# A retention layer with a token mixer: batch 0 loaded pair by pair, with two tokens to a partition

## Chip, cores, metric

The kernel runs on one core of a Trainium2 chip. The metric is the device time of one execution in microseconds (us), as the median of several runs. Lower is better.

## What is computed

The inputs q, k and v have the shape (4 batches, 8 heads, 768 tokens, 64 features) in float32. The first half is a retention recurrence. In each head a 64x64 state decays by a factor gamma that depends on the head, takes up the outer product of k and v of the token, and is read out with q:

```python
for t in range(S):
    state = gamma * state + einsum('bhd,bhe->bhde', k[:, :, t], v[:, :, t])
    y[:, :, t] = scale * einsum('bhd,bhde->bhe', q[:, :, t], state)
```

The heads of a token are then laid side by side to a row x of 512 features, and the second half mixes tokens within a batch and projects:

```python
wq, wk = x @ w_q, x @ w_k                       # 512 -> 64
W_tok  = scale2 * einsum('bsd,btd->bst', wq, wk)
mixed  = einsum('bst,btd->bsd', W_tok, x)
out    = maximum(mixed, 0) @ w_out              # 512 -> 512
```

The mixing needs no S x S matrix: z = wk^T x is a 64x512 matrix for each batch, and mixed = wq z. So no output of a batch can be made before z is complete, that is before all tokens of that batch have passed through the first half.

## The kernel before

**Chunks, pairs, batches.** The 768 tokens of a batch are six chunks of 128 (C), and two chunks are a pair (p). There are twelve pairs in all, 0 to 2 for batch 0, 3 to 5 for batch 1, and so on (NP = 3 pairs to a batch). Inside a chunk the recurrence is done as attention: scores from k and q, a causal mask, and a product with v ("intra"). Between chunks the state carries over ("inter"). The decay is folded into k and q when they are cast to bf16: k is multiplied by gamma^-t (table `fk`), q by gamma^t (table `fq`).

**Steps.** Each step is a small function, with the pair and often the chunk as its arguments:

- `ck`, `cq`, `cv` (lines 300 to 313, with `decay`, 286): cast a pair of k, q or v from its staging tile to bf16, with the decay for k and q. This runs on DVE (V), POOL (P) or ACT (A).
- `trk`, `trq` (315, 330): eight TensorE transposes of a pair of k or q into one PSUM bank; `ekT`, `eqT` evict them to SBUF.
- `sc` (349): scores of a chunk, eight matmuls that contract over the 64 features of one head (64 rows of the array, 128 columns), two heads side by side on the two row halves. `eat` (365) evicts them, with the mask on DVE, or without it on ACT followed by `msk` (380) on POOL.
- `st` (420): adds a chunk's k^T v to the state in PSUM, four matmuls on 128 rows. `es` (433) evicts the state to bf16.
- `in` (390) and `ia` (405): inter and intra part of y in one PSUM bank; `ia` has eight matmuls on 128 rows. `ex` (448) evicts y as x.
- `xt`, `exT`, `wqk`, `ew` (455 to 496): transpose x, project it with w_q and w_k, evict.
- `za`, `zm`, `ez` (515 to 525): z of a batch, twelve matmuls in a column-tiled form (64 output rows each).
- `mx`, `r`, `pj`, `eo` (527 to 565): mix, relu, output projection (line 553, four matmuls of 512 columns), eviction, and then the store of the pair.
- `W`, `WO`: cast the weights.

**The order.** Nothing is scheduled by the compiler. The string `ORDER` (line 18) is walked token by token (line 583) and lays down the instructions of each engine in that order. In `sc.1.0@2+3` the numbers are pair, chunk and PSUM banks; `ekT.5:A` runs on ACT. An engine takes its instructions strictly in order, so that a step that waits holds back all that stands behind it on the same engine. `fill.150` puts 150 matmuls on a zero tile, which nobody reads, ahead of the next step on PE (`fresh`, line 277). The order before has fills of 150, 36, 5 and 3.

**The loads.** All DMAs are issued by SP, in program order. `load` (155) brings one tensor of a whole batch (1.57 MB). k and v come with token n*128+p on partition p, in rows of 256 bytes; q with the tokens 2p and 2p+1 of a pair on partition p, in rows of 512 bytes. At the start come k, q, v of batch 0, w_q, w_k, k of batch 1, w_out, q and v of batch 1. The third cast of a tensor of batch b issues its load for batch b+2 (`release`, 186) into the same staging tile. In the old order all of these loads stand before the first store on SP.

Of the kernel before, what the change touches and what calls it, by code (L numbers as in the profile page):

```python
# [9 lines left out]
FP32 = mybir.dt.float32  # L10
# [16 lines left out]
ew.0:V ia.2.0 es.2.0:V xt.1@6 ex.2.0:A exT.1:V fill.5 in.2.1@4
ia.2.1 ck.4:P ex.2.1:V wqk.1@5 WO:V trk.5@4 ew.1:A xt.2@6
ekT.5:A za.0@5 ck.3:P exT.2:V trk.4@2 wqk.2@4 ekT.4:A ew.2:V
trk.3@6 zm.0 ekT.3:V ez.0:A mx.0@4+5 cq.3:P mx.1@6+2 r.0.0:A  # L30
r.0.1:V r.1.1:A r.1.0:V mx.2@4+5 pj.0.1@2 cq.5:P trq.3@6 eo.0.1:A
eqT.3:V pj.0.0@2 cq.4:P trq.5@6 r.2.0:A sc.3.0@0+1 eqT.5:V r.2.1:A
pj.1.0@4 cv.3:A eat.3.0:V cv.5:P trq.4@5 cv.4:A pj.2.0@6 eqT.4:V
eo.1.0:V st.3.0 eo.0.0:A ia.3.0@5 eo.2.0:V es.3.0:A sc.3.1@0+1 sc.4.0@2+3
ex.3.0:A pj.2.1@4 eat.3.1:V in.3.1@5 eo.2.1:A st.3.1 eat.4.0:V ia.3.1
es.3.1:A fill.3 sc.4.1@0+1 pj.1.1@4 ex.3.1:A eat.4.1:V ck.6:P st.4.0
in.4.0@5 es.4.0:A xt.3@6 eo.1.1:V sc.5.0@0+1 exT.3:V st.4.1 ck.7:P
sc.5.1@2+3 es.4.1:A eat.5.0:V wqk.3@4 st.5.0 ew.3:A in.5.0@6 es.5.0:V
ia.4.0 ck.8:P ia.5.0 ex.4.0:A trk.7@4 eat.5.1:V ex.5.0:A in.4.1@5
ia.4.1 in.5.1@6 ex.4.1:A ekT.7:V ia.5.1 cq.6:P trk.8@2 ex.5.1:A  # L40
xt.4@4 ekT.8:V xt.5@5 exT.4:A trk.6@6 exT.5:V cq.7:P trq.6@2
ekT.6:V wqk.4@4 eqT.6:V wqk.5@5 ew.4:A cq.8:P trq.7@4 ew.5:A
cv.6:A sc.6.1@0+1 eqT.7:V sc.6.0@2+3 zm.1@5 eat.6.1:V cv.8:A cv.7:P
trq.8@4 st.6.0 eat.6.0:V ez.1:A sc.7.0@0+1 eqT.8:A mx.3@5+6 es.6.0:V
r.3.1:A sc.7.1@2+3 ia.6.0@4 r.3.0:A eat.7.1:V in.6.1@6 st.6.1 ex.6.0:A
ia.6.1 pj.3.0@5 es.6.1:A ex.6.1:V ck.10:P in.7.0@4 ck.9:P eo.3.0:A
st.7.0 xt.6@6 es.7.0:A eat.7.0:V exT.6:V sc.8.1@0+1 sc.8.0@2+3 in.7.1@5
eat.8.0:V st.7.1 trk.10@6 es.7.1:A ia.7.0 ia.7.1 eat.8.1:V ex.7.0:A
st.8.0 wqk.6@2 ex.7.1:A ck.11:P trk.9@4 es.8.0:A ew.6:V in.8.0@5
ekT.9:V ia.8.0 in.8.1@2 ex.8.0:A ia.8.1 pj.3.1@4 ekT.10:V cq.9:P  # L50
ex.8.1:A trk.11@5 eo.3.1:A xt.7@6 ekT.11:V xt.8@4 cq.10:P exT.7:V
trq.9@2 exT.8:A wqk.7@5 eqT.9:V wqk.8@4 cq.11:P ew.7:A cv.11:A
trq.10@6 ew.8:V mx.4@5+2 eqT.10:V sc.9.0@0+1 r.4.0:A zm.2@4 eat.9.0:V
r.4.1:A cv.10:P trq.11@5 cv.9:A sc.10.1@2+3 ez.2:A eqT.11:V sc.9.1@0+1
pj.4.0@6 eat.9.1:V st.9.0 eo.4.0:A pj.4.1@4 eat.10.1:V es.9.0:A sc.11.0@0+1
eo.4.1:A mx.5@5+6 eat.11.0:V sc.11.1@2+3 r.5.0:A in.9.1@4 st.9.1 ia.9.0@5
es.9.1:A ia.9.1 r.5.1:V sc.10.0@0+1 ex.9.0:A eat.11.1:V st.10.0 pj.5.0@6
es.10.0:A ex.9.1:A in.10.1@5 eat.10.0:V st.10.1 eo.5.0:A pj.5.1@2 es.10.1:A
eo.5.1:A xt.9@4 in.11.0@6 exT.9:V st.11.0 ia.11.0 es.11.0:A ia.10.1
ex.11.0:V wqk.9@4 ex.10.1:A in.11.1@2 ew.9:A ia.11.1 mx.6@5+6 ex.11.1:A  # L60
in.10.0@4 r.6.0:V ia.10.0 r.6.1:A xt.11@2 ex.10.0:A pj.6.1@5 exT.11:V
wqk.11@4 eo.6.1:A mx.7@6+2 ew.11:V xt.10@5 r.7.0:A r.7.1:V pj.6.0@4
exT.10:V pj.7.0@6 eo.6.0:A wqk.10@4 eo.7.0:A pj.7.1@5 ew.10:A mx.8@4+6
eo.7.1:A za.3@2 r.8.0:A zm.3 r.8.1:V ez.3:A pj.8.0@4 eo.8.0:A
mx.9@5+6 pj.8.1@2 r.9.1:V r.9.0:A pj.9.0@4 eo.8.1:A mx.10@5+6 eo.9.0:A
pj.9.1@2 r.10.1:V r.10.0:A mx.11@4+5 eo.9.1:A pj.10.0@6 r.11.1:V r.11.0:A
pj.11.1@2 eo.10.0:V pj.10.1@5 eo.11.1:A pj.11.0@4 eo.10.1:V eo.11.0:A
""".split()

# [5 lines left out]
def kernel(  # L75
# [9 lines left out]
):  # L85

# [65 lines left out]

    staged = {}

    def load(name, b):
        src = {"k": k, "q": q, "v": v}[name]
        if name == "q":
            t = buf("q_st", b % 2, [H, NP, 2, D], FP32)
            nc.sync.dma_start(
                out=t.rearrange("p h n j d -> p (h n) (j d)"),  # L160
                in_=src[b].rearrange("h (n p j) d -> p (h n) (j d)", p=128, j=2),
            )
        else:
            t = buf(name + "_st", b % 2, [H, NCH, D], FP32)
            nc.sync.dma_start(
                out=t.rearrange("p h n d -> p (h n) d"),
                in_=src[b].rearrange("h (n p) d -> p (h n) d", p=128),
            )
        staged[name, b] = t
# [459 lines left out]
```

## Time and profile before

| | us |
|---|---|
| median of 3 runs (lowest, highest) | 110.6 (109.92, 110.98) |
| the profiled execution | 110.53 |
| its span, from first to last instruction | 108.7 |
| PE busy in the span | 95.0 (87%) |
| DVE, ACT, POOL busy | 74.4, 61.2, 52.6 |
| mean granted TensorE clock | 0.972 |
| DMA | 26.66 MB, 245 GB/s on average |

Busy times are sums of an engine's instructions. PE is the matmul part of TensorE and PEld its weight loads; matmuls are pipelined, so that a single one shows a longer duration than the step from one to the next. The chain that ended last follows the last instruction back to what released it at each step, and its durations are the steps from one to the next. SPq rows are DMA issues on SP's queue; their duration is the time for which the issue holds SP, and the DMA view gives the time from issue to landing.

### The profile page before, as it was taken

To read this page: it belongs to the slowest core of one execution; us is meant where nothing else is said; L and a number is where in the kernel's file an instruction comes from. 1 tells how busy PE (TensorE), PEld (TensorE's weight loads), DVE (VectorE), ACT (ScalarE), POOL (GpSimd) and SP (SyncE) were. 2 spreads that over 40 slices of the span, in tenths; PEclk is the share of its full clock that TensorE was granted. 3 is DMA by queue.
4 is the path that set the end of the run, shared out by engine and by line. 5 is a ranking of instruction groups with operands and counts; after the bars stand their busy time and mean duration, and the time that the engine had idled before them with its cause. 6 is when DMAs were issued, how large, how long until landed. Compare 5 with 4: busy or idle time off the path is not lost.

```text
span 108.7 us, 3189 instructions
## 1 busy us (share of the span) xinstructions
PE 95.0 (87%) x1362; PEld 72.7 (67%) x1362; DVE 74.4 (68%) x97; ACT 61.2 (56%) x112; POOL 52.6 (48%) x46
## 2 busy tenths in 40 slices
PE   6999984669997679999999899999999999999920
PEld 6999982449895435666998678888675965633400
DVE  2007999998599544999976999966998556132520
ACT  6000003494427146985785985868789974767420
POOL 6607355299696993185999059999000000000000
PEclk9999999995999999999999999999999999999995
DMA  1989995599999979699998899798013220444472
GB/s 19 320 266 346 353 337 148 154 328 236 383 390 344 330 233 332 193 369 342 301 319 258 284 347 304 241 409 344 18 71 128 111 87 0 193 193 193 193 295 91
DMA packets 19020, 26.66 MB, mean 245 GB/s; under 512 B 1472, under 2 KB 13760, under 8 KB 19008
## 3 DMA queue, kind: packets, MB, share of 16 engines
q1 hardware_dynamic: 19008, 26.48, 73.5%
q8 instruction: 10, 0.16, 0.6%
q14 instruction: 2, 0.02, 0.0%
HBM read 20.19 MB, written 6.29 MB: 243 GB/s over the span
## 4 chain that ended last, share of the span: by engine, by line
PE 69%; DVE 18%; ACT 6%; issue 2%; DVEq 0%; ACTq 0%
PE bank_ps L553 14%; PE bank_ps L280 11%; PE duo_ps L553 5%; PE bank_ps L473 5%; PE duo_ps L355 5%; PE state_ps L424 4%; PE bank_ps L411 4%; PE bank_ps L396 4%; DVE at L371 4%; DVE qs L288 4%; PE bank_ps L532 3%; PE bank_ps L336 3%; DVE wout_sb L146 3%; PE bank_ps L460 3%; PE bank_ps L319 2%; DVE kT L146 2%
## 5 line engine op out<-in xcount | busy, mean ns | idle before, releaser
L288 POOL TENSOR_TENSOR ks<-k_st,fk 128x1024 bf16<-128x1024 f32 x10 | 19.9, 2004 | 14.7 <-PE state_ps L424 6.6
L371 DVE TENSOR_TENSOR at<-duo_ps,cmask 128x1024 bf16<-128x1024 f32 x21 | 25.0, 1216 | 0.1
L288 POOL TENSOR_TENSOR qs<-q_st,fq 128x1024 bf16<-128x1024 f32 x10 | 19.8, 2008 | 4.2 <-DMA q_st<-in_q_dram 4.2
L553 PE MATMUL bank_ps<-wout_sb,relu 128*128 128x512 bf16 x72 | 18.2, 380 | 0.1
L280 PE MATMUL bank_ps<-warm 128*128 128x128 bf16 x191 | 14.0, 247 | 1.0 <-DVE warm L196 1.0
L280 PEld LDWEIGHTS <-warm 128*128 128x128 bf16 x194 | 13.8, 113 | 1.0 <-DVE warm L196 1.0
L553 PEld LDWEIGHTS <-relu 128*128 128x128 bf16 x96 | 8.1, 97 | 9.1 <-issue 1.2
L144 ACT CAST x<-bank_ps 128x512 bf16<-128x512 f32 x18 | 10.4, 590 | 3.7 <-PE bank_ps L411 3.4
L144 ACT CAST s_sb<-state_ps 64x256 bf16<-64x256 f32 x28 | 10.3, 367 | 3.9 <-PE state_ps L424 2.8
L355 PE MATMUL duo_ps<-qT,kT 64*128 64x128 bf16 x192 | 8.8, 219 | 2.7 <-ACT at L144 1.5
L547 DVE TENSOR_SCALAR relu<-bank_ps 128x512 bf16<-128x512 f32 x8 | 5.4, 689 | 8.3 <-PE bank_ps L532 8.3
L144 ACT COPY o<-bank_ps 128x512 f32<-128x512 f32 x13 | 7.6, 586 | 6.1 <-PE bank_ps L553 6.1
L144 ACT COPY qT<-bank_ps 128x1024 bf16<-128x1024 bf16 x2 | 2.0, 1018 | 14.3 <-PE bank_ps L336 14.3
L355 PEld LDWEIGHTS <-kT 64*128 64x128 bf16 x192 | 6.0, 94 | 5.0 <-issue 3.7
L288 DVE TENSOR_TENSOR ks<-k_st,fk 128x1024 bf16<-128x1024 f32 x2 | 4.1, 2076 | 7.1 <-DMA k_st<-in_k_dram 7.1
L545 ACT ACTIVATE relu<-bank_ps 128x512 bf16<-128x512 f32 x13 | 7.6, 604 | 1.8 <-PE duo_ps L553 0.7
L411 PE MATMUL bank_ps<-vs,at 128*128 128x64 bf16 x176 | 8.6, 198 | 0.0
L424 PE MATMUL state_ps<-vs,ks 128*128 128x128 bf16 x80 | 8.2, 228 | 0.1
L336 PEld LDWEIGHTS <-qs 128*128 128x128 bf16 x96 | 5.8, 98 | 3.5 <-POOL qs L288 1.3
L411 PEld LDWEIGHTS <-at 128*128 128x128 bf16 x192 | 7.9, 101 | 0.3 <-DVE at L371 0.2
L473 PE MATMUL bank_ps<-xT,wq_sb 128*128 128x256 bf16 x44 | 6.6, 273 | 1.7 <-DVE xT L146 1.5
L336 PE MATMUL bank_ps<-identity,qs 128*128 128x128 bf16 x80 | 6.1, 220 | 1.9 <-POOL qs L288 1.1
(75 smaller groups left out, 164.5 us busy)
## 6 DMA issues: line engine op xcount, KB each, us to landing
out_dram<-o SPq DMA_DIRECT2D x11, 512.0 KB, 2.6
wout_stage<-in_moe_w_out_dram SPq DMA_DIRECT2D x1, 1024.0 KB, 10.1
out_dram<-o SPq DMA_DIRECT2D x2, 256.0 KB, 2.3
wq_stage<-in_moe_w_q_dram SPq DMA_DIRECT2D x1, 128.0 KB, 9.4
wk_stage<-in_moe_w_k_dram SPq DMA_DIRECT2D x1, 128.0 KB, 2.9
k_st<-in_k_dram SPq DMA_DIRECT2D x4, 0.2 KB, 10.5
q_st<-in_q_dram SPq DMA_DIRECT2D x4, 0.5 KB, 12.0
v_st<-in_v_dram SPq DMA_DIRECT2D x4, 0.2 KB, 12.0
```

What stands on the lines that cost most here:

```text
L144: nc.scalar.copy(out=out, in_=in_)
L146: ENGINES[e].tensor_copy(out=out, in_=in_)
L280: nc.tensor.matmul(out=ps[:, 0:128], lhsT=warm, rhs=warm, start=True, stop=True)
L288: ENGINES[e].tensor_tensor(out=t, in0=staged[name, p // NP][shape].rearrange(order), in1=table.to_broadcast([128, 2, H, D]), op=ALU.mult,)
L336: nc.tensor.transpose(ps[:, :, hp, j, :], pairs[p]["qs"][:, j, 2 * hp : 2 * hp + 2, :].rearrange("p x d -> p (x d)"), identity,)
L355: nc.tensor.matmul(out=ps[:, x, hp, :], lhsT=st["kT"][rows(x), c, hp, :], rhs=st["qT"][rows(x), c, hp, :], start=(hp == 0), stop=(hp == HP ...
L371: nc.vector.tensor_tensor(out=t.rearrange("p x hp t -> p (x hp) t"), in0=ps.rearrange("p x hp t -> p (x hp) t"), in1=cmask.rearrange("p o ...
L411: nc.tensor.matmul(out=st["y", c][:, h * D : (h + 1) * D], lhsT=st["at", c][:, x, hp, :], rhs=st["vs"][:, c, h, :], start=(first and h == ...
L424: nc.tensor.matmul(out=state_ps[:, hp, :], lhsT=st["ks"][:, c, 2 * hp : 2 * hp + 2, :].rearrange("p x d -> p (x d)"), rhs=st["vs"][:, c, 2 ...
L473: nc.tensor.matmul(out=ps[:, 0 : 2 * C].rearrange("p (j c g) -> p j c g", j=2, c=2), lhsT=wq_sb[:, a].rearrange("p o h -> p (o h)"), rhs=s ...
L545: nc.scalar.activation(out=dst, in_=st["mx"][half], func=ACT.Relu)
L553: nc.tensor.matmul(out=ps, lhsT=st["relu", a // 2][:, a % 2, j], rhs=wout_sb[:, a, :], start=(a == 0), stop=(a == NDM - 1),)
```

## The change

Only batch 0 changes its form.

- **Loads of batch 0.** Nine loads of one pair of one tensor each (0.52 MB, rows of 512 bytes) stand in place of three, in the order of the new list `FIRST`, all on SP. k and v now also have the tokens 2p and 2p+1 of a pair on partition p. The staging tiles of batch 0 are laid out pair by pair.
- **Batch 0's arithmetic.** A chunk is now the half c of the partitions, with two tokens j on each. So the second argument of `sc` and `ia` means half of the heads (i), with both chunks, rather than a chunk. `sc` has 16 matmuls on 64x64 tiles of the array (64 features by 64 tokens), `ia` has 16 that contract over 64 partitions, and `st` has 8 on 64 partitions. The k table for this form is `fk2`, one more exponential on ACT. The mask is `cmask2`, made at the start on POOL; all evictions of scores of batch 0 are masked on DVE, and `msk` is no longer called.
- **Batches 1 to 3** keep their loads and their matmuls on 128 rows.
- **The order** is written anew as a whole. It has one fill of 100. On SP the store of pair 0 (after `eo.0.0`) and that of pair 1 (after `eo.1.1`) now stand before the loads of q and v of batch 3, which follow `cq.4` and `cv.4`.

```diff
-fill.150 ck.1:V ck.0:P ck.2:V trk.1@4 trk.0@5 ekT.1:V trk.2@6
...
+fill.100 ck.0:V trk.0@4 cq.0:V ekT.0:A trq.0@5 cv.0:P eqT.0:A
+st.0.0 ck.1:V sc.0.0@0+1 es.0.0:A sc.0.1@2+3 in.0.1@4 eat.0.0:V st.0.1
+cq.1:P eat.0.1:V trk.1@5 es.0.1:A ekT.1:V ia.0.0@6 ia.0.1 trq.1@5
+ck.2:P ex.0.1:A ex.0.0:V cq.2:P xt.0@4 trk.2@6 exT.0:A eqT.1:V
+trq.2@2 cv.1:P sc.1.0@0+1 eqT.2:A in.1.0@4 ekT.2:V eat.1.0:V st.1.0
+cv.2:P sc.1.1@2+3 es.1.0:V sc.2.1@0+1 eat.2.1:V st.1.1 in.1.1@5 W:P
+es.1.1:A ia.1.0 eat.1.1:V st.2.0 sc.2.0@0+1 es.2.0:A ia.1.1 eat.2.0:V
+in.2.1@6 ex.1.1:A wqk.0@2 ex.1.0:A in.2.0@5 ew.0:A ia.2.0 ia.2.1
+xt.1@4 ex.2.0:A ex.2.1:V xt.2@5 exT.1:V wqk.1@4 exT.2:V ck.5:P
+wqk.2@5 ew.1:A ew.2:A za.0@4 ck.4:P trk.5@6 zm.0 ekT.5:V
+ez.0:A WO:V mx.0@4+5 mx.1@6+2 ck.3:P r.0.0:A r.0.1:A r.1.1:V
+r.1.0:A trk.4@4 pj.0.1@5 ekT.4:A trk.3@6 eo.0.1:A pj.1.0@2 eo.1.0:A
+ekT.3:V pj.0.0@4 cq.5:P pj.1.1@5 eo.0.0:A mx.2@4+6 eo.1.1:A cq.3:P
+r.2.0:V trq.5@2 r.2.1:A eqT.5:V pj.2.1@4 sc.5.0@0+1 cq.4:P eat.5.0:V
...
+r.5.0:A exT.8:V sc.9.0@2+3 cq.11:P trq.10@4 eat.9.1:V pj.5.0@5 eqT.10:V
+pj.5.1@6 cv.9:A cv.11:P cv.10:P eat.9.0:V st.9.0 eo.5.0:A sc.10.1@0+1
...
+FIRST = "k0 q0 v0 k1 q1 k2 q2 v1 v2".split()
...
+    def load_pair(name, n, queue):
+        queue.dma_start(
+            out=stage(name, 0)[:, n],
+            in_=SRC[name][0, :, n * 2 * C : (n + 1) * 2 * C, :].rearrange(
+                "h (p j) d -> p h (j d)", j=2
+            ),
+        )
...
-    for name in "kqv":
-        load(name, 0)
+    for part in FIRST:
+        load_pair(part[0], int(part[1]), nc.scalar if part.endswith("A") else nc.sync)
...
+    nc.scalar.activation(out=fk2, in_=lq, func=ACT.Exp, scale=-1.0)
...
+    for t, base in ((cmask2, 0), (cmask2_b, C)):
+        nc.gpsimd.memset(t, 1.0)
+        for j in range(2):
+            nc.gpsimd.affine_select(
...
+    nc.gpsimd.tensor_copy(out=cmask2[64:128], in_=cmask2_b[64:128])
...
+        if p < NP:                                   # sc
+            for m in range(HP):
+                hp, j = 2 * i + m // 2, m % 2
+                for x in range(2):
+                    for c in range(2):
+                        nc.tensor.matmul(
+                            out=ps[rows(c), x, m, :],
+                            lhsT=st["kT"][rows(x), c, hp, j * G : j * G + G],
+                            rhs=st["qT"][rows(x), c, hp, :],
...
+        if p < NP:                                   # eat
+            nc.vector.tensor_tensor(
+                out=t.rearrange("p x (hi j) t -> p (x hi) (j t)", j=2),
+                in0=ps.rearrange("p x (hi j) t -> p (x hi) (j t)", j=2),
+                in1=cmask2.rearrange("p o j t -> p o (j t)").to_broadcast([128, HP, 2 * C]),
...
+        if p < NP:                                   # ia
+            for m in range(HP):
+                hp, j = 2 * i + m // 2, m % 2
+                for x in range(2):
+                    h = 2 * hp + x
+                    for c in range(2):
+                        nc.tensor.matmul(
+                            out=st["y", c][:, h * D : (h + 1) * D],
+                            lhsT=st["at", i][rows(c), x, m, :],
+                            rhs=st["vs"][rows(c), j, h, :],
...
+        parts = [(rows(c), j) for j in range(2)] if p < NP else [(slice(0, 128), c)]   # st
         for hp in range(HP):
...
+            for i, (ps, slot) in enumerate(parts):
+                nc.tensor.matmul(
+                    out=state_ps[:, hp, :],
+                    lhsT=st["ks"][ps, slot, 2 * hp : 2 * hp + 2, :].rearrange("p x d -> p (x d)"),
+                    rhs=st["vs"][ps, slot, 2 * hp : 2 * hp + 2, :].rearrange("p x d -> p (x d)"),
```

More of the change, by code (lines that the diff above doesn't have):

```diff
@@ L27 @@
[L27 to L57, printed above, removed]
```

243 lines of the change are left out of this document (134 added, 109 removed).

## The prediction, made before the changed kernel was built

> **What bounds the kernel now.** I read the page's slices first, then busy time by stretch, then the timelines of the DMA queue and of the start, then the chain that ended last. The slices (2.72 us each):
>
> ```profile
> span 108.7 us, 3189 instructions
> ...
> PE   6999984669997679999999899999999999999920
> ...
> PEclk9999999995999999999999999999999999999995
> ...
> GB/s 19 320 266 346 353 337 148 154 328 236 383 390 344 330 233 332 193 369 342 301 319 258 284 347 304 241 409 344 18 71 128 111 87 0 193 193 193 193 295 91
> ```
>
> The sixes and sevens of PE stand in the first 40 us; the early nines are warm matmuls. Two stretches, each from its own answer:
>
> ```profile
> 39.87:104.03 64.16, 62.91 (x880) 43.89 (x879) 46.45 (x59) 47.00 (x91) 26.33 (x16) 1.00 0.67 228
> ```
>
> ```profile
> 17.60:21.00 3.40, 1.79 (x32) 1.40 (x33) 3.28 (x4) 1.22 (x2) 0.24 (x1) 1.00 0.43 103
> 21.00:24.40 3.40, 2.22 (x44) 1.60 (x44) 3.40 (x4) 2.87 (x3) 3.34 (x3) 0.96 1.06 318
> 24.40:27.80 3.40, 3.31 (x42) 3.20 (x41) 2.51 (x4) 1.66 (x4) 2.96 (x4) 0.54 0.98 264
> ```
>
> (Columns: length, then PE, PEld, DVE, ACT, POOL busy, granted clock, DMA share, GB/s.) From 39.87, the first output projection, to 104.03, where the last one ends, PE works 62.91 of 64.16 us: TensorE sets the time there, and a change that keeps its work can save nothing. Before 39.87, PE waits. What for, in the timeline of the start and of the DMA queue:
>
> ```profile
> 8.71 4.07 DVE L288 TENSOR_TENSOR ks<-k_st,fk 128x1024 bf16<-128x1024 f32 x2 [7.11 <-DMA k_st<-in_k_dram]
> ...
> 14.90 2.95 POOL L288 TENSOR_TENSOR qs<-q_st,fq 128x1024 bf16<-128x1024 f32 x1 [3.20 <-DMA q_st<-in_q_dram]
> ```
>
> ```profile
> 7.46 2.89 SPq L165 DMA_DIRECT2D v_st<-in_v_dram  x1
> 10.40 7.37 SPq L177 DMA_DIRECT2D wq_stage<-in_moe_w_q_dram  x1
> 17.82 1.14 SPq L178 DMA_DIRECT2D wk_stage<-in_moe_w_k_dram  x1
> ...
> 59.77 3.30 SPq L165 DMA_DIRECT2D v_st<-in_v_dram  x1
> ```
>
> The DMA view gives from issue to landing, for the first v load and then (a second answer) for the last:
>
> ```profile
> v_st<-in_v_dram SPq DMA_DIRECT2D x1, 0.2 KB, 11.9
> ```
>
> ```profile
> v_st<-in_v_dram SPq DMA_DIRECT2D x1, 0.2 KB, 12.0
> ```
>
> All of k lands at 8.7, all of q at 14.9, all of v at 7.46 + 11.9 = 19.36; three pairs stand before each. So the opening is bound by loads as wide as a batch, then by the three pairs' evictions.
>
> **What pair loads give.** Slice one moves nearly nothing, so bytes flow from 2.7 us: nine pairs' worth by 19.36, 1.85 us for each 0.52 MB. At the best slices' 345 GB/s it would be 1.52, with no landing lag. I take 1.85 (measured for the same bytes). In the order of FIRST: k0 4.55, q0 6.4, v0 8.25, k1 10.1, q1 11.95, k2 13.8, q2 15.65, v1 17.5, v2 19.35. The last byte comes no sooner; the first pair's tensors come 4 to 11 us earlier. SP has nine issues in place of three: at wk's 1.14 us they need 10.3 of the 16.7 us that the bytes take, so SP doesn't set the pace unless it blocks (rival 4).
>
> PE is behind its fills first:
>
> ```profile
> 1.04:4.45 3.41, 3.41 (x33) 3.41 (x34) 1.00 0.59 170
> 4.45:7.87 3.42, 3.42 (x42) 3.42 (x41) 1.00 0.97 292
> 7.87:8.60 0.73, 0.73 (x17) 0.73 (x15) 1.00 0.89 297
> ```
>
> 92 by 8.60 and 43 ns for each further one: 100 fills end near 9.0, when pair 0 is cast. The dropped fills (36, 5 and 3) lay in waits, except 0.17 us at 48.4. Dense durations, from the chain that ended last and then from the groups by form:
>
> ```profile
> 48.54 0.33 PE duo_ps L355 x8
> 48.87 0.97 PE bank_ps L553 x4
> 49.84 0.22 PE state_ps L424 x4
> 50.06 0.22 PE bank_ps L396 x4
> 50.29 0.45 PE bank_ps L460 x8
> ...
> 51.73 0.54 PE bank_ps L473 x4
> 52.27 0.23 PE bank_ps L483 x8
> ...
> 54.24 0.23 PE bank_ps L411 x8
> ...
> 75.54 0.78 PE bank_ps L506 x12
> ...
> 98.76 0.33 PE bank_ps L532 x4
> ```
>
> ```profile
> L371 DVE TENSOR_TENSOR at<-duo_ps,cmask 128x1024 bf16<-128x1024 f32 x21 | 25.0, 1216 | 0.1
> ...
> L144 ACT CAST x<-bank_ps 128x512 bf16<-128x512 f32 x18 | 10.4, 590 | 3.7 <-PE bank_ps L411 3.4
> ...
> L146 DVE COPY kT<-bank_ps 128x1024 bf16<-128x1024 bf16 x9 | 5.9, 685 | 1.2 <-PE bank_ps L319 1.0
> ...
> L146 POOL CAST vs<-v_st 128x1024 bf16<-128x1024 f32 x4 | 4.6, 1150 | 0.0
> ...
> L438 DVE TENSOR_TENSOR s_sb<-state_ps,dmask 128x512 bf16<-128x512 f32 x6 | 4.1, 684 | 0.7 <-ACT x L144 0.5 <-PE state_ps L424 0.2
> ...
> L146 DVE CAST wout_sb<-wout_stage 128x2048 bf16<-128x2048 f32 x1 | 2.9, 2890 | 0.0
> ```
>
> ```profile
> 51.48 1.91 POOL L288 TENSOR_TENSOR ks<-k_st,fk 128x1024 bf16<-128x1024 f32 x1 [1.35 <-PE state_ps L424]
> ```
>
> **What 64-row tiles cost.** Only batch 0 pays. A score step has 16 matmuls of 64x64 for 8 of 64x128, an intra step 16 for 8 with half the rows, a state step 8 for 4. No row shows a 64x64 tile. From below: no dearer, 0.33 for a score step (four tiles at once). From above: the column-tiled z row, 0.78/12 = 65 ns each, 1.04. I take 0.50 (31 ns each, nearest to the x8 rows), intra 0.46 and state 0.44, twice their rows, as a state step's halves share a tile row; intra's lower end is 0.23. DVE gets six masked evictions at 1.22 in batch 0 where three were split over ACT and POOL; I count them on the path. POOL's extra mask (two memsets, four selects, a copy; about 1.8 us by the start's small POOL steps) hides before v0 lands at 8.25; without that cover it would delay v0's cast by 1.8. The extra exponential on ACT hides before k0.
>
> *A rule against it:* the z row is slow per matmul, and the Trainium skill, TensorEngine Tiling (Array Packing), Restrictions, says that column tiling turns the fast weight load off. The rule agrees with that row; by its price, estimated from TensorE: Matmul & The Clock Gate (LDWEIGHTS) at 64/1.2 = 53 ns a load, a score step is 0.85 and the forecast about 1.4 us later.
>
> **The path through batch 0.** q2 lands at 15.65; POOL, after cv.0, cq.1 and ck.2, is free at 15.8; cq.2 takes 1.9 (POOL alone; 2.95 beside a DVE cast), to 17.7; trq.2 to 18.2. sc.1.0 stands behind trq.2 on PE, so pair 1 waits for pair 2's q: that is the wait that replaces the old one. From there DVE leads: sc.1.0 to 18.7, then four evictions and es.1.0, 4 x 1.22 + 0.68, to 24.3. Beside it cv.1 and cv.2 end at 19 and 20.4, before st.1.0 and st.2.0 ask. In.2.1, wqk.0, in.2.0, ia.2.0 and ia.2.1 end at 25.8; ex.2.1 26.6; xt.2 27.1; exT.2 (behind exT.1) 28.0; wqk.2 28.8; za.0 and trk.5 29.8; zm.0 and ez.0 30.5. Then mx.0, which stood at:
>
> ```profile
> 38.31 0.44 PE bank_ps L532 x4
> ...
> 39.89 1.02 PE duo_ps L553 x4
> ```
>
> WO now starts behind ekT.5, 30.5 to 33.4, and pj.0.1 waits for it: 33.5 at full clock. ck.5 hides: batch 1's k lands by 26.
>
> PE from 9 to 24 is no denser than in the two stretches before 24.40, after which the granted clock was 0.54 for 3.4 us. With doubled PE steps from sc.1.0 to sc.2.1 (2.2 us) the sequence is 1.9 late, and with the later ones 2.2: first projection 35.7. I take one such window on half of this, +1.2: **34.7** (33.5 to 35.7).
>
> **From there to the end.** The same steps as from 39.87, plus trk.3 (0.45), which the old order had done: 34.7 + 64.16 + 0.45 = 99.3 for the last matmul. Behind it 108.7 - 104.03 = 4.67 of eviction and store, unchanged: span 104.0. The profiled execution's 110.53 has 1.83 outside its span: **105.8**. That execution is 0.07 under the runs' median of 110.6, so no correction.
>
> **The loads behind.** On SP the old order put every load before the first store. Now store 0 and store 1 (eo.0.0, eo.1.1) stand before the q and v loads of batch 3: 1.05 MB, 3.05 us at 345 GB/s. Against that, slices 16.3 to 21.7 ran at 150 GB/s, where wq's issue blocked 7.37 us behind the first v load of 256-byte rows: 0.8 MB moved in 5.4 us, 3 us lost; with 512-byte rows before it I count 2.3 back (0 to 3.7). The last v lands at 59.77 + 12.0 - 2.3 + 3.05 = 72.5. Behind st.9.0 the order has 24.4 us of dense PE (12 projections, 11.2; 6 mx, 2.0; 4 wqk, 3.1; 3 xt and trq.11, 1.8; the rest 6.3), so that load would allow the last matmul at 72.5 + 1.15 + 24.4 = 98.1. It is 1.2 us off the path: little cover.
>
> **Rivals.**
>
> 1. *No throttled window.* For: the stretches before 24.40 themselves had 1.00 and 0.96. Against: the one after. First projection 33.5, time 104.6. The Trainium skill, TensorE: Matmul & The Clock Gate, Part 1, asks an idle window of about 3.4 us for half clock; read strictly it gives this rival, as no such idle stretch is left; here the 0.54 row followed windows that were half busy, so the trace does not bear it out.
>
> 2. *Dear tiles.* Score steps at 1.04 on four path places (+2.2), with some of them in a throttled window (+0.9): first projection 37.8, time 108.9. For: the z row. Against: row-tiled L355 at 41 ns.
>
> 3. *The last loads lead.* No stream time comes back: last v at 74.8, last matmul 100.4, time 106.9. For: store 0 and 1 in front. Against: the hole at 150 GB/s.
>
> 4. *Slower: small loads don't stream.* Nine loads in place of three, each with an issue and a landing. q2 is the seventh, so each microsecond more per load moves the path by seven. At 2.53 us a load the gain is gone, at 2.69 it is 1% slower. The nearest row for a small load landing alone:
>
> ```profile
> wq_stage<-in_moe_w_q_dram SPq DMA_DIRECT2D x1, 128.0 KB, 9.4
> wk_stage<-in_moe_w_k_dram SPq DMA_DIRECT2D x1, 128.0 KB, 2.9
> ```
>
> At 2.9 each, q2 lands at 23.0, 7.35 later: 113.2. Against it: wq, issued at 10.40 with 9.4 to landing, and wk landed 0.9 us apart.
>
> **How the numbers follow.** Forecast 105.8: 0.52; rival 1 104.6: 0.14; rival 2 108.9: 0.14; rival 3 106.9: 0.10; rival 4 113.2: 0.10. One per cent is 1.1 us, about what a measurement tells: faster is under 109.5, slower over 111.7. Faster: 0.50 + 0.14 + 0.08 + 0.10 = 0.82; same 0.02 + 0.05 + 0.01 = 0.08; slower 0.10. The range leaves out rival 4 and the tails: from 103.6 (rival 1 with tiles at their lower bound) to 109.6 (rival 2 with the dearer half clock).
>
> **What would show it.** Right: ck.0 on DVE at 4.5 to 5.5; trk.0 near 9.0; trq.2 near 18; the first L553-kind projection at 33.5 to 35.7; PE about 98% busy after it; last matmul near 99; no idle before cv.9 of over 1 us. Wrong: q2 landing after 18, score steps over 0.8 us, a first projection past 37, or PE waiting on q_st or v_st of batch 3.

## The result, and the profile after

| | before | after |
|---|---|---|
| median of 4 runs (lowest, highest), us | 110.79 (109.92, 111.09) | 106.59 (105.73, 107.44) |
| ratio to before, 95% interval | | 0.961 (0.949 to 0.973) |
| profiled execution, its span | 110.53, 108.7 | 107.44, 105.5 |
| PE busy | 95.0 | 91.2 |

The change makes the kernel 4% faster here (two repeats further down have ratios of 0.973 and 0.979). The forecast was 105.8, in a range of 103.6 to 109.6. The profiled execution is the longest of the four, and every row below is from that one. Ratios leave out runs that were over 1.5% above the fastest of the same kernel and medians do not, so that a ratio can differ by a per cent or two from that of two medians.

The page of the changed kernel, its slices of 2.64 us:

```profile
span 105.5 us, 3225 instructions
...
PE   6997953899979989799979999978999999999950
...
PEclk9999999999999999999999999999999999999999
...
GB/s 28 317 346 352 337 274 277 333 259 308 372 346 276 255 101 330 263 343 233 336 223 325 357 365 273 327 320 235 421 365 16 6 0 0 199 0 207 385 235 174
```

The 150 GB/s hole that followed the first v load is gone (277, 333 and 259 stand there now), and the clock is full throughout. A new hole stands at slice 15, 101 GB/s. PE has sevens and eights between 29 and 74 us, where before one eight stood behind 40.

The start, first in DVE's timeline of the changed kernel, then in POOL's, then SP's (start, duration, what, and what ended the idle time before):

```profile
4.91 1.23 DVE L330 TENSOR_TENSOR ks<-k_st,fk 128x1024 bf16<-128x1024 f32 x1 [3.31 <-DMA k_st<-in_k_dram]
6.40 1.23 DVE L330 TENSOR_TENSOR qs<-q_st,fq 128x1024 bf16<-128x1024 f32 x1 [0.26 <-DMA q_st<-in_q_dram]
```

```profile
7.95 1.04 POOL L150 CAST vs<-v_st 128x1024 bf16<-128x1024 f32 x1 [0.95 <-DMA v_st<-in_v_dram]
12.50 1.90 POOL L330 TENSOR_TENSOR qs<-q_st,fq 128x1024 bf16<-128x1024 f32 x1 [3.52 <-DMA q_st<-in_q_dram]
14.36 1.90 POOL L330 TENSOR_TENSOR ks<-k_st,fk 128x1024 bf16<-128x1024 f32 x1
16.22 1.90 POOL L330 TENSOR_TENSOR qs<-q_st,fq 128x1024 bf16<-128x1024 f32 x1
```

```profile
13.60 1.66 SPq L197 DMA_DIRECT2D wq_stage<-in_moe_w_q_dram  x1
...
23.70 6.02 SPq L181 DMA_DIRECT2D v_st<-in_v_dram  x1
30.18 7.93 SPq L181 DMA_DIRECT2D k_st<-in_k_dram  x1
...
54.52 5.35 SPq L641 DMA_DIRECT2D out_dram<-o  x2
60.09 0.71 SPq L181 DMA_DIRECT2D q_st<-in_q_dram  x1
61.26 4.82 SPq L181 DMA_DIRECT2D v_st<-in_v_dram  x1
```

The pairs arrive one by one and their casts follow: k0 at 4.9, q0 at 6.4, v0 at 7.95; q2's cast, behind two others in POOL's queue, runs from 16.2 to 18.1. The issue of w_q holds SP for 1.66, for 7.37 before. The last rows show stores 0 and 1 holding SP from 54.52 to 59.87, right ahead of the last q and v loads.

Busy time by stretch in the changed kernel, one stretch ahead of those that were shown of before, these three, and the one from its first output projection to the end of the last (length; PE, PEld, DVE, ACT, POOL; clock, DMA share, GB/s):

```profile
14.20:17.60 3.40, 1.71 (x24) 1.34 (x24) 1.98 (x4) 1.60 (x2) 3.40 (x3) 1.00 1.06 295
17.60:21.00 3.40, 2.61 (x68) 2.02 (x69) 1.87 (x4) 1.01 (x1) 3.31 (x5) 1.00 1.04 305
21.00:24.40 3.40, 2.94 (x74) 2.38 (x74) 3.17 (x4) 1.86 (x5) 0.84 (x2) 1.00 0.96 230
24.40:27.80 3.40, 3.16 (x72) 2.63 (x70) 2.16 (x4) 1.75 (x4) 3.40 (x2) 1.00 1.01 372
...
32.36:101.67 69.31, 65.52 (x890) 45.15 (x887) 46.95 (x61) 47.53 (x86) 34.13 (x21) 1.00 0.70 234
```

PE is denser in the two stretches from 17.60 (2.61 and 2.94 for 1.79 and 2.22), and the one behind them is at full clock, not 0.54. The sparse stretch has moved ahead, to 14.20 (1.71). But the last stretch, 64.16 us before, is 69.31: PE idles 3.8 us in it, where it idled 1.25.

Pieces of the chain that ended last in the changed kernel:

```profile
18.18 0.62 PE duo_ps L358 x8
18.80 0.38 PE duo_ps L392 x16
...
61.26 13.64 DMA v_st<-in_v_dram
74.92 1.05 ACT vs L148
76.02 0.38 PE state_ps L494 x4
```

The first two are trq.2 and the score step behind it. The third is the last load of all. It stands on the chain for 13.64 us; in the chain of before no load of batch 3 stood. And two rows of the timelines of PE and DVE, the first projection and the cast of w_out:

```profile
32.34 1.02 PE L623 MATMUL bank_ps<-wout_sb,relu 128*128 128x512 bf16 x4
```

```profile
30.61 1.22 DVE L150 CAST wout_sb<-wout_stage 128x2048 bf16<-128x2048 f32 x1
```

So the opening gained 7.5 us (39.87 to 32.34), and 5.2 of it were given back behind it (64.16 to 69.3).

### The profile page after: what moved, and what is told of

It is laid out like the page before. It is cut to its first block, busy times and chain, and to the rows that moved or that the text cites. A ratio compares the mean times of both kernels' runs of the same rounds, so it can differ in the third digit from the quotient of the medians.

```text
span 105.5 us, 3225 instructions
## 1 busy us (share of the span) xinstructions
PE 91.2 (86%) x1384; PEld 67.1 (64%) x1384; DVE 65.8 (62%) x91; ACT 61.9 (59%) x113; POOL 55.6 (53%) x56
## 2 busy tenths in 40 slices
DMA packets 24494, 26.68 MB, mean 253 GB/s; under 512 B 1568, under 2 KB 20000, under 8 KB 24480
## 4 chain that ended last, share of the span: by engine, by line
PE 40%; DMA 20%; ACT 16%; DVE 6%; SPq 5%; POOL 5%; issue 4%; DVEq 0%; ACTq 0%; POOLq 0%
DMA v_st<-in_v_dram 13%; PE bank_ps L623 12%; DMA q_st<-in_q_dram 7%; ACT s_sb L148 6%; PE duo_ps L623 4%; PE bank_ps L358 4%; SPq L184 4%; POOL qs L330 4%; ACT x L148 3%; PE bank_ps L543 3%; PE state_ps L494 2%; PE bank_ps L576 2%; ACT vs L148 2%; PE bank_ps L530 2%; POOL ks L330 2%
## 5 line engine op out<-in xcount | busy, mean ns | idle before, releaser
L426 DVE TENSOR_TENSOR at<-duo_ps,cmask 128x1024 bf16<-128x1024 f32 x18 | 21.4, 1217 | 1.5 <-PE duo_ps L403 1.4
L150 POOL CAST vs<-v_st 128x1024 bf16<-128x1024 f32 x9 | 9.1, 1039 | 2.9 <-DMA v_st<-in_v_dram 2.4
L494 PE MATMUL state_ps<-vs,ks 128*128 128x128 bf16 (+1 forms) x100 | 8.9, 218 | 1.4 <-ACT s_sb L148 0.9
L150 DVE COPY xT<-bank_ps 128x1024 bf16<-128x1024 bf16 x9 | 6.1, 684 | 4.5 <-PE bank_ps L530 4.4
L419 DVE TENSOR_TENSOR at<-duo_ps,cmask 128x1024 bf16<-128x1024 f32 x6 | 7.2, 1220 | 2.5 <-PE duo_ps L392 2.5
L148 ACT COPY kT<-bank_ps 128x1024 bf16<-128x1024 bf16 x4 | 4.1, 1018 | 7.9 <-PE bank_ps L358 7.9
L150 DVE COPY kT<-bank_ps 128x1024 bf16<-128x1024 bf16 x8 | 5.5, 685 | 5.0 <-PE bank_ps L358 4.7
L358 PE MATMUL bank_ps<-identity,ks 128*128 128x128 bf16 x96 | 7.4, 219 | 1.2 <-POOL ks L330 0.8
L494 PEld LDWEIGHTS <-ks 128*128 128x128 bf16 (+1 forms) x100 | 6.2, 96 | 3.4 <-issue 1.7
L313 PE MATMUL bank_ps<-warm 128*128 128x128 bf16 x100 | 7.3, 247 | 1.0 <-DVE warm L209 1.0
L313 PEld LDWEIGHTS <-warm 128*128 128x128 bf16 x100 | 7.1, 114 | 1.0 <-DVE warm L209 1.0
```

What stands on the lines that cost most here:

```text
L148: nc.scalar.copy(out=out, in_=in_)
L150: ENGINES[e].tensor_copy(out=out, in_=in_)
L313: nc.tensor.matmul(out=ps[:, 0:128], lhsT=warm, rhs=warm, start=True, stop=True)
L358: nc.tensor.transpose(ps[:, i, hp, :] if whole(name, p // NP) else slots[:, :, hp, i, :], pairs[p][name + "s"][:, i, 2 * hp : 2 * hp + 2, ...
L419: nc.vector.tensor_tensor(out=t.rearrange("p x (hi j) t -> p (x hi) (j t)", j=2), in0=ps.rearrange("p x (hi j) t -> p (x hi) (j t)", j=2), ...
L426: nc.vector.tensor_tensor(out=t.rearrange("p x hp t -> p (x hp) t"), in0=ps.rearrange("p x hp t -> p (x hp) t"), in1=cmask.rearrange("p o ...
```

## The experiments

Theories for the 5.2 us. **L**: the last v load leads the end, late because two stores stand in front of it on SP. **P**, set against it in the first expectations: no load leads, and the end follows the first projection by some 65 us of PE work. **N**, which later took P's place: the new order itself waits more for evictions. For the gain the theory is that **pair loads** with 512-byte rows bring batch 0 early; the rival, that the new order or the clock does most of it. Ratios are to the kernel before, timed beside each kernel on the same chip, with 95% intervals.

**The changed kernel again.** No edit; the yardstick for the next three.

> The changed kernel as it is, as the base of this group: 105.7 to 107.4 us by both theories. Theory L (the loads lead): after the first projection near 32.4 us the end is set by the stream of later loads, so POOL and ACT show waits on k_st, q_st and v_st of batches 1 to 3, and PE idles 2 us or more between the first projection and 76 us. Theory P (PE leads): these waits are cover, and the end follows from the first projection plus about 65 us of PE work; then PE would idle under 1 us there.

Measured: 107.66 (107.01 to 109.13), ratio 0.973 (0.963 to 0.983). Its profiled execution has the first projection at 31.72 and the last v cast at 75.98. The clock was half in one slice of it near 14 us, without a later projection. From its first projection to that cast PE idled 4.4 us, where L had 2 or more and P under 1. Its runs differ by 2%, those of the next kernel by 0.4%.

**Stores 0 and 1 behind the last loads.** A store is kept back until v of batch 3 has been asked for.

```diff
-                store(p)
+                if ("v", B - 1) in staged:
+                    store(p)
+                else:
+                    late.append(p)
+        if ("v", B - 1) in staged:
+            for p in late:
+                store(p)
+            late.clear()
```

> The stores of pairs 0 and 1 are issued behind the q and v loads of batch 3 on SP; nothing else changes. Theory L: the last v load lands about 3 us sooner (near 72) and the last matmul ends 1.5 to 2.3 us sooner: 104.3 to 105.1 us. Theory P: 106.6 within 0.4.

Measured: 105.82 (105.60 to 105.98), ratio 0.962 (0.955 to 0.968); 1.8 us under the changed kernel on the same chip. In its timeline the last v cast waits for no DMA, and in its stretch from the first to the last projection PE still idles 2.8 us:

```profile
71.74 1.06 ACT L148 CAST vs<-v_st 128x1024 bf16<-128x1024 f32 x1
```

```profile
31.60:99.62 68.02, 65.18 (x890) 45.12 (x887) 46.98 (x61) 47.54 (x87) 34.05 (x21) 1.00 0.72 240
```

L holds for this part: the cast comes 3 to 4 us sooner and the end 2 to 3. But 68.02 remains where the forecast had 64.61. So L isn't all, and with PE idle for 2.8 us P doesn't hold either.

**cq.2 on DVE.** Takes POOL's queue out of the way of trq.2, the step that the prediction put on the path.

```diff
-ck.2:P ex.0.1:A ex.0.0:V cq.2:P xt.0@4 trk.2@6 exT.0:A eqT.1:V
+ck.2:P ex.0.1:A ex.0.0:V xt.0@4 trk.2@6 exT.0:A eqT.1:V cq.2:V
```

> The cast of pair 2's q moves from POOL to DVE, behind eqT.1, where DVE idles for over a microsecond; POOL's three casts in a row then no longer hold trq.2. Both theories: trq.2 near 17.2 instead of 18.2 and the first projection 0.6 to 1.0 us sooner. Theory L: the end doesn't move, 106.6 within 0.4. Theory P: it moves by the same, 105.6 to 106.0 us.

Measured: 108.05 (106.64 to 108.72), ratio 0.975 (0.962 to 0.987). The cast runs at 16.51 behind DVE's own evictions, trq.2 at 17.78, the first projection at 31.93: nothing gained at the start, since DVE's queue took the place of POOL's, and nothing at the end, where the last v cast stood at 74.76. Both theories had expected an earlier first projection, and both missed.

**k and v of batches 1 to 3 in 512-byte rows.** Here their tokens are in another order than the reference's, so batches 1 to 3 of the result differ; the work is the same.

```diff
-            n, src = NCH, SRC[name][b].rearrange("h (n p) d -> p (h n) d", p=128)
+            n, src = NP, SRC[name][b].rearrange("h (n p j) d -> p (h n) (j d)", p=128, j=2)
```

> k and v of batches 1 to 3 are fetched as rows of 512 bytes (two neighbouring tokens to a partition, so that these batches work on their tokens in another order than the reference); same bytes, same instructions on every compute engine. Theory L: the loads follow one another at about 4.7 us instead of 5.5, the last v load lands 4 us or more sooner, and PE alone sets the end: 103.3 to 104.5 us. Theory P: 106.6 within 0.4.

Measured: 106.00 (105.83 to 106.75), ratio 0.965 (0.957 to 0.973), less of a gain than expected. The last v cast came at 73.61, only 1.3 sooner than in the first profile, and still waited 1.81 for its load: longer rows help, and the stores in front remain.

**Batch 0 in three whole loads again**, all with 512-byte rows; the arithmetic and the order are those of the changed kernel.

```diff
-        order = "n h e" if b == 0 else "h n e"
+        order = "h n e"
...
-    for part in FIRST:
-        load_pair(part[0], int(part[1]), nc.scalar if part.endswith("A") else nc.sync)
+    for name in "kqv":
+        load(name, 0)
```

> Batch 0 comes in three whole loads (k, q, v, rows of 512 bytes) instead of nine, all else as in the changed kernel. Theory L (arrivals set the opening, the last v load sets the end): pair 0's scores wait for all of q (about 13 us), DVE takes pair 0's evictions 4 us later, the first projection moves by 1.5 to 2.5 us to 33.5 to 34.5; the last v cast stays within 1 us of 75 us, so the end stays within 0.7 us of the changed kernel. Rival (the pair loads are the whole gain): the first projection goes back to 37 us or later and the time to within 1 us of the kernel before.

Measured: 115.04 (113.65 to 115.53), ratio 1.057 (1.030 to 1.083). Here my expectation was wrong by some 7 us. The rival was right that without the pair loads the whole gain is gone, but not in size: it had the time of the kernel before within 1 us, and this is 5 us above it. POOL's timeline and the clock of this kernel say why:

```profile
17.87 1.04 POOL L150 CAST vs<-v_st 128x1024 bf16<-128x1024 f32 x1 [10.85 <-DMA v_st<-in_v_dram]
18.88 1.90 POOL L330 TENSOR_TENSOR qs<-q_st,fq 128x1024 bf16<-128x1024 f32 x1
```

```profile
PEclk9999755558999999999999999999999999999997
```

The order has cv.0 at the head of POOL's queue, and v is the last of three loads: cq.1, whose data had been there for 4 us (q's first cast ran on DVE at 13.73), waits behind it. PE waits with it, the clock falls to half for four slices (11 us), and the first projection comes at 40.69. An order written for early pairs needs the early pairs.

**Pair loads with the old matmul form.** Batch 0 has one token to a partition again, so the k and v pairs come in 256-byte rows, each as two DMAs (15 loads in all), with all matmuls on 128 rows.

```diff
+        if name != "q":
+            for c in (2 * n, 2 * n + 1):
+                queue.dma_start(
+                    out=stage(name, 0)[:, c],
+                    in_=SRC[name][0, :, c * C : (c + 1) * C, :].rearrange("h p d -> p h d"),
+                )
+            return
...
-        if p < NP:
+        if p < 0:
...
-        parts = [(rows(c), j) for j in range(2)] if p < NP else [(slice(0, 128), c)]
+        parts = [(rows(c), j) for j in range(2)] if p < 0 else [(slice(0, 128), c)]
```

> Batch 0 in the old form: k and v by chunk with rows of 256 bytes (15 loads), all matmuls of scores, intra and state on 128-row operands, in the changed order. Theory L with cheap tiles (a score step took 0.38 to 0.42 us in both forms): first projection within 0.7 us of 32, end within 0.7 us of the changed kernel. Rival (the 64-row form is dear): first projection 1 to 2 us sooner than 31.6. Rival (256-byte rows are dear at the start): first projection 1 to 2 us later than 32.4.

Measured: 110.58 (110.27 to 111.27), ratio 1.024 (1.014 to 1.035). Its slices and its packets:

```profile
GB/s 48 277 272 229 230 184 298 232 256 326 115 374 376 359 340 169 337 259 357 348 338 283 310 372 281 335 252 287 288 379 142 2 6 0 193 0 134 362 273 202
DMA packets 30733, 26.67 MB, mean 246 GB/s; under 512 B 13952, under 2 KB 26240, under 8 KB 30720
```

Where the changed kernel had 317 to 352 GB/s, then 274, this one has 277, 272, 229, 230 and 184, with 13952 packets under 512 bytes (after: 1568). The first projection stands at 34.86. The clock has a part in that: it was 0.87 and 0.63 in the stretches from 14.20 and 17.60, where the changed kernel's was full. Nor is 110.58 the opening's alone: the last v load came late, its cast at 78.19. So here pair loads pay only with two tokens to a partition (the number of loads went up with the shorter rows, and the two aren't told apart); the smaller tiles on TensorE are the price, and cost little. The Trainium skill, DMA: Bandwidth & Descriptors, Specifications, gives 512 bytes as the shortest transfer at line rate; these slices agree.

**Stores behind, and each later k and v load cut in four by heads**, to see whether the big loads of 256-byte rows hold SP and the stream.

```diff
+            for h in range(0, H, 2):
+                nc.sync.dma_start(
+                    out=raw(name, b).rearrange("p (m e) -> p m e", m=H * NCH)[
+                        :, h * NCH : (h + 2) * NCH
+                    ],
+                    in_=SRC[name][b, h : h + 2].rearrange("h (n p) d -> p (h n) d", p=128),
+                )
+            return
```

> As with the stores of pairs 0 and 1 behind the last loads (105.8), and each k and v load of batches 1 to 3 issued as four DMAs of two heads, the same rows and bytes. If SP's hold behind one large load of 256-byte rows makes the holes between loads: last v lands 1 to 3 us sooner than 69 us, POOL's waits on k_st shrink, 104.3 to 105.2 us. If not (the straggling DMA engine makes them): 105.8 within 0.4.

Measured: 109.72 (108.87 to 111.77), ratio 1.015 (0.999 to 1.030): 3.9 us longer than the kernel with the stores behind alone on the same chip (105.82), the opposite of what was expected.

```profile
DMA packets 52431, 26.69 MB, mean 246 GB/s; under 512 B 38720, under 2 KB 47936, under 8 KB 52416
```

The page has 52431 packets for 24494: by these counts cut loads move as single rows and whole ones don't. The last v cast came at 77.27 behind a load, though no store stood in front of it. L's link from a late load to the end is confirmed from the other side.

**Stores behind and 512-byte rows together** (the edits of the second and fourth experiments; the tokens of batches 1 to 3 are in the other order as there). If L were all, the stretch from first to last projection would now be as long as the forecast had it.

> Both: the stores behind the last loads and k and v of batches 1 to 3 in rows of 512 bytes (their tokens in another order than the reference, same instructions on the compute engines). Theory L: no load is late any more, the last v lands before 67 us, PE alone sets the end: last matmul at the first projection plus 65 to 66 us, 103.0 to 104.3 us. Rival (the new order has waits of its own among PE, DVE and ACT): 105.2 to 106.

Measured: 106.29 (105.81 to 106.82), ratio 0.984 (0.974 to 0.994), nearer to the rival's 105.2 to 106 than to L's 104.3. No load of batch 3 is late, and the stretch is as long as with the stores behind alone:

```profile
31.80:99.86 68.06, 65.22 (x890) 45.13 (x887) 46.92 (x60) 47.61 (x86) 34.03 (x21) 1.00 0.67 241
```

Sooner loads buy nothing more: 68.06 is the order's own length. N holds for this part.

**The new opening with the old order behind it** (two tries). `ORDER` is kept up to `mx.1@6+2 ck.3:P`, and behind a short seam the tokens of the old order follow. The first try's seam, and the second's (lines wrapped anew):

```diff
 ez.0:A WO:V mx.0@4+5 mx.1@6+2 ck.3:P
-r.0.0:A r.0.1:A r.1.1:V r.1.0:A trk.4@4 pj.0.1@5 ekT.4:A trk.3@6 eo.0.1:A pj.1.0@2
+cq.3:P r.0.0:A r.0.1:A r.1.1:V r.1.0:V trk.4@4 ekT.4:A trk.3@6 ekT.3:V mx.2@4+5 pj.0.1@2
```

```diff
-r.0.0:A r.0.1:A r.1.1:V r.1.0:A trk.4@4 pj.0.1@5 ekT.4:A trk.3@6 eo.0.1:A pj.1.0@2
+cq.3:P r.0.0:A r.0.1:A r.1.1:V r.1.0:V trk.4@4 pj.0.1@5 ekT.4:A trk.3@6 eo.0.1:A cq.5:P
```

> The changed opening up to the first two mix steps, and from there the order of the kernel before (its loads all ahead of its stores). Theory N (behind the first projection the new order has 3.4 us of waits of its own, among PE, ACT and DVE, that the old order does not have): first projection near 32, last matmul 64.6 to 66.5 us behind it, 102.3 to 104.0 us. Rival (those waits belong to the opening's early end, with loads and evictions that can't keep up whatever the order): last matmul 68 us behind, 105.8 or more.

> The spliced order with its seam mended: the first projection stands ahead of trk.3 again, the second mix of pair 2 and pair 0's other projection ahead of the steps that wait for batch 1's q. Theory N (the old order behind the opening has fewer waits of its own): first projection near 32, last matmul 65 to 67 us behind it (65.2 in the first splice), 103.0 to 105.0 us. Rival (the loads of batches 1 and 3 make the late part wait whatever the order): 105.5 or more.

Measured: 106.54 (104.58 to 108.83), ratio 0.962 (0.948 to 0.976), for the first, and 106.15 (104.15 to 109.09), ratio 0.956 (0.942 to 0.970), for the second. The first one's stretch from first to last projection:

```profile
34.55:99.73 65.18, 64.16 (x881) 44.52 (x879) 46.51 (x59) 46.94 (x91) 29.55 (x18) 0.98 0.72 241
```

65.18, and 66.10 in the second, for 68.06. But this measure flatters the splice, since both seams were mine and poor: the first projection slid to 34.55 and 36.49. From the first mix step, up to which these orders are the same, to the last eviction it is 69.49 and 68.91, for 69.61 with the stores behind alone: as a whole nothing was gained. What the seam doesn't touch shows in PE's rows of the first score step of batch 1 (`sc.3.0`), before and in the two tries:

```profile
42.97 0.40 PE L355 MATMUL duo_ps<-qT,kT 64*128 64x128 bf16 x8
```

```profile
38.67 0.40 PE L398 MATMUL duo_ps<-qT,kT 64*128 64x128 bf16 x8
```

```profile
41.62 0.40 PE L398 MATMUL duo_ps<-qT,kT 64*128 64x128 bf16 x8
```

From there to the last eviction (104.03, 99.73, 102.59) it is 61.06, 61.06 and 60.97: the old order takes its own time behind the new opening too, whenever it starts. That is N, and it speaks against the rival, that the loads hold up the late part whatever the order. The loss is in the seam, 8.43 and 7.94 us from the first mix step to `sc.3.0`, for 4.66 before, where two k transposes (0.9) had been done by then.

The clock was half in the slice of the first one's seam (33.7 to 36.3), and in the second it was half for three slices (19 to 27 us) of the opening, which is that of the changed kernel. That a clean seam would gain 3 us (69.61 against 4.66 + 0.9 + 61.06) is an estimate and not shown; the fastest run (104.15) was the lowest of any kernel here, beside a 109.09 of the same kernel.

**Stores behind, and the changed kernel, once more**, on other chips.

> The changed kernel with the stores of pairs 0 and 1 behind the last loads, once more, as the base for the spliced order: 105.8 us within 0.4, last matmul 68 us behind the first projection.

> The changed kernel once more, as the base for the mended splice on the same chip: 106.0 to 107.7 us, the last matmul 26.7 to 26.8 us behind the start of the first cast of batch 3's v on ACT.

Measured: 105.82 (105.60 to 106.67), ratio 0.969 (0.962 to 0.976), and 107.20 (106.26 to 109.29), ratio 0.979 (0.969 to 0.989). The third profile of the changed kernel has its last load later still:

```profile
76.64 1.05 ACT L148 CAST vs<-v_st 128x1024 bf16<-128x1024 f32 x1 [3.27 <-DMA v_st<-in_v_dram]
```

**What all profiles say together.** Three starts from each timeline: the first projection, ACT's cast of the last v (in brackets its wait for the load), and the eviction behind the last projection.

| kernel | first projection | last v cast | last eviction | from projection | from cast |
|---|---|---|---|---|---|
| before | 39.87 | 76.32 (none) | 104.03 | 64.16 | 27.71 |
| old order behind, first try | 34.55 | 72.01 (none) | 99.73 | 65.18 | 27.72 |
| old order behind, second try | 36.49 | 74.88 (none) | 102.59 | 66.10 | 27.71 |
| after | 32.34 | 74.92 (1.39) | 101.69 | 69.35 | 26.77 |
| after, second profile | 31.72 | 75.98 (1.39) | 102.74 | 71.02 | 26.76 |
| after, third | 31.55 | 76.64 (3.27) | 103.41 | 71.86 | 26.77 |
| cq.2 on DVE | 31.93 | 74.76 (1.31) | 101.52 | 69.59 | 26.76 |
| 512-byte rows | 31.50 | 73.61 (1.81) | 100.38 | 68.88 | 26.77 |
| old matmul form | 34.86 | 78.19 (1.55) | 104.96 | 70.10 | 26.77 |
| loads cut in four | 32.12 | 77.27 (2.00) | 104.05 | 71.93 | 26.78 |
| stores behind | 31.57 | 71.74 (none) | 99.62 | 68.05 | 27.88 |
| stores behind, again | 31.77 | 71.94 (none) | 99.83 | 68.06 | 27.89 |
| stores behind, 512-byte rows | 31.79 | 71.98 (none) | 99.86 | 68.07 | 27.88 |
| three whole loads | 40.69 | 80.88 (none) | 108.76 | 68.07 | 27.88 |

With the new order the last eviction starts 26.77 after the last v cast wherever that cast waited for its load, and 68.06 after the first projection wherever it didn't: two constants, each to 0.01 us, over kernels that differ in their loads, rows and opening, and over several chips. So the end is the later of the two, and a late load and the order's own length don't add up. That settles how the 5.2 us divide in the first profile: 68.06 - 64.16 = 3.9 for the order, and 69.35 - 68.06 = 1.3 for the load. The three profiles of the changed kernel are each the longest run of their group, so that the load costs less in most of its runs; by the medians on one chip it is 1.8 (107.66 against 105.82).

The clock, which the rival for the gain named, has a part in it. Beside the experiments there are 36 runs of the kernel before. Three had a mean granted clock of 0.99 or more, and took 107.68, 108.94 and 109.09 us; the others have a median of 110.24. Of the changed kernel's 16 runs 12 had such a clock, with a median of 107.32. So between runs at full clock the gain looks nearer 1.6 us than 3: a part of what the change brings would be that it mostly goes without the half-clock window of before. Three runs are few, and no experiment moved the clock alone, so this is argued and the share stays open.

Where the order waits shows in the chain that ended last. With the stores behind, some of its pieces:

```profile
39.68 1.05 ACT vs L148
40.72 0.91 ACT qT L148
41.64 0.26 ACT s_sb L148
41.92 0.38 ACT s_sb L148
...
43.53 0.58 ACT x L148
44.11 0.26 ACT s_sb L148
...
61.25 1.02 DVE at L426
62.39 1.22 DVE at L426
63.60 0.60 DVE s_sb L508
64.20 1.14 DVE at L426
...
78.67 1.01 ACT xT L148
```

From 39.68 to 47.36 ACT leads, with a v cast, a qT and then state and x evictions one behind the other; one PE step of 0.40 stands between them. Summed over the pieces of the chain from first to last projection, PE has 45.0 us, ACT 12.0 and DVE 8.0; before, 53.7, 2.5 and 7.6 (old order behind the new opening: 55.0, 1.8 and 7.6). The new order lets ACT lead for 10 us more. Which token is to blame isn't settled; no run moved one.

## Why the prediction was right, and where its steps were not

The time and the sign were right, by errors of both signs; that 105.8 came so close is luck. Against the profiled execution the forecast is 1.64 short: -2.34 in the opening (32.36 for 34.7), +4.72 from there to the last matmul (69.33 for 64.61), -0.86 in the tail (3.81 for 4.67) and +0.11 outside the span. Why the tail is shorter stays open.

- **Arrivals: right.** k0 4.9 for 4.55, q0 6.4, v0 7.95 for 8.25. It took 1.85 us a pair; at the start the pairs came 1.5 apart, and one load of q1 came 1.5 late (12.4; in the other two profiles of this kernel 10.9). Rival 4 (small loads don't stream) fell; in the old matmul form, with 256-byte rows, part of it came true.
- **The path through batch 0: right.** POOL's queue stood ahead of trq.2 as said, which ran from 18.18 to 18.80; the prediction had it end at 18.2, so it was 0.6 late, for the most part by the late q1. The fills ended at 8.3 for 9.0. w_out's cast began at 30.61 for 30.5.
- **Tiles: taken dearer than they were.** A score step took 0.38 on the chain and 0.42 in its row for the 0.50 taken, 24 to 26 ns a matmul. By the Trainium skill's rule that column tiling goes without the fast weight load (TensorEngine Tiling (Array Packing), Restrictions and Gotchas), at the price that the prediction estimated for it, it would have been 0.85; the trace doesn't bear that out for 64x64 tiles. Rival 2 fell.
- **The half-clock window: not there in this profile, and by chance.** The prediction took one, at +1.2, since "PE from 9 to 24 is no denser". From 17.60 it was denser (2.61 and 2.94), but the stretch ahead was as sparse as before's (1.71), and full clock followed it. Of eleven profiles with this opening (the changed kernel's three, both with the stores behind, cq.2 on DVE, 512-byte rows with and without stores behind, loads cut in four, both splices) eight show full clock up to the first projection. Two have one such stretch (0.60 and 0.59 from 14.20), with no later projection in the second profile of the changed kernel; and the second splice has the window in full, behind stretches like those of the profile above:

```profile
14.20:17.60 3.40, 1.84 (x24) 1.36 (x24) 2.01 (x4) 1.56 (x2) 3.40 (x2) 1.00 1.08 296
17.60:21.00 3.40, 3.14 (x40) 2.38 (x44) 1.23 (x1) 1.01 (x1) 3.31 (x5) 0.53 0.97 285
```

  Its first projection came at 36.49. So rival 1 was right for this execution, the forecast's window comes in some others of the same opening, and PE's density (1.71 against 1.84) doesn't tell which.
- **WO at 2.89: mis-sized.** It took 1.22, -1.7. The price was read from a row where POOL cast k beside it, and here POOL was idle (more on that below). Clock and WO alone make -2.9. Behind the cast, which ended at 31.83, the prediction had 0.1 to the projection; it took 0.5, with trk.4 in between (31.85 to 32.34).
- **"The same steps as from 39.87, plus trk.3 (0.45)": this step failed.** It counted the work and not the order. The work was nearly right: mx.2 also stands behind the first projection now (0.37, the chain), fills worth 0.17 no longer do. But "PE works 62.91 of 64.16" belonged to the old order of tokens, and the new order was taken over with it at no cost, though the change said that the order was written anew as a whole. The runs show 68.06 for this order, wherever no load is late: 3.45 more than the 64.61 forecast. The matmuls on PE in the stretch say the same of the work: with the stores behind, 59 k transposes for 48 before and 40 of mixing for 37, no fills for 3, and every other count alike. PE's busy time rose all the same, from 62.91 to 65.18, and its idle time from 1.25 to 2.84; a matmul's row is longer than the step to the next, so that each stop adds to the busy time as well (this reading is argued).
- **The loads behind: the last load did lead, as in rival 3, but not for its reason.** Stream time did come back: the first k load of batch 1 landed at 24.0, before at 26.5, and with the stores behind the last v landed at 68.9 and 70.0 (57.09 + 11.8, 59.38 + 10.6), for 71.8 before and the 69.5 that the prediction has without its stores. What was too small is the price of the two stores, 3.05 by their bytes at 345 GB/s. With them in front the last v landed at 74.9, 75.9 and 76.6, 5 to 8 us later than behind them (with 512-byte rows 73.6 and 67.9). They held SP for 5.35 us in the profile (54.52 to 59.87), which fits; that it is this hold and not the bytes is argued. Rival 3's 74.8 is right only by luck. The path behind the load was given 24.4 us of dense PE; the steps took 25.67 from st.9.0 (76.02) to the end (101.69). So the load was on the path, not "1.2 us off" it, and worth 1.3 to 3.8 us in three profiles (69.35, 71.02 and 71.86 against 68.06).

A better kernel than both was on the way: with the stores behind the last loads it took 105.82 on each of two chips (ratios 0.962 and 0.969). The changed kernel took 107.66 on the first of them and 107.20 on a third (0.973 and 0.979), though the four runs of the result reach down to 105.73. That is a per cent or so, and a narrower spread.

## What to carry to other kernels

A dense stretch in a profile prices that stretch's order, not its work: when an order is rewritten, read the new one's evictions engine by engine, or allow for a few per cent. A load that is issued late behind stores on the same queue sets the end long before it looks like it, so keep stores behind the last load, or price both, with the time for which the store holds the queue and not only its bytes. And here small loads paid only with long rows: choose the layout that makes 512-byte rows first, and the tile form second.

## What the runs showed of the hardware

- **A DVE cast waits for POOL's.** In each of the ten profiles in which POOL was casting k or q when it began, the w_out cast on DVE ended 1.1 us after that POOL cast, whenever it began: before, it began at 32.33, POOL ended at 34.13, it ended at 35.22; in the second profile of the changed kernel 29.89, 30.58, 31.66; with the stores behind, again, 30.04, 30.62, 31.72; in the third profile of the changed kernel 29.83, 30.11, 31.20, from these rows of POOL and DVE:

```profile
24.49 5.62 POOL L330 TENSOR_TENSOR ks<-k_st,fk 128x1024 bf16<-128x1024 f32 x3 [3.53 <-DMA k_st<-in_k_dram]
```

```profile
29.83 1.37 DVE L150 CAST wout_sb<-wout_stage 128x2048 bf16<-128x2048 f32 x1
```

  Alone it took 1.22. That is one engine blocked until the other is done, not two slowed down, as the Trainium skill says of the port that they share (SBUF — State Buffer, Who interferes with whom); 2.89 was 1.8 of waiting. POOL waits in its turn: where another of its casts stood behind, the row of three took 6.6 us for 5.62 (three whole loads, old matmul form, second splice).
- **A load cut up by heads is not the same load.** Whole, the 1.57 MB loads of 256-byte rows left 1568 packets under 512 bytes in the page; in four parts 38720, and the loads came later. The 256-byte pair loads of the old matmul form moved row by row as well (13952).
- **64x64 tiles with 128 moving columns** took 24 to 26 ns each: a score step of 16 is 0.38, where 8 of the 64x128 form took 0.33.
- **One load of an identical program can land nearly 2 us later in one run than in another** (74.9, 75.9 and 76.6 for the last v). The changed kernel shows it in its time, since that load leads; with the stores behind (68.9 and 70.0) it didn't show.
- **The same opening ran at full clock in some executions and at half clock in others**: 1.71 of 3.40 us of PE work from 14.20 on was followed by a granted clock of 1.00, 1.84 by 0.53.
